# A linear-attention block times a GEGLU FFN: sums of fp32r passes recorded as three parts in free order, with a new schedule

## The chip, the core and the metric

The kernel runs on one core of one Trainium2 chip. The metric is the device time of one execution in microseconds (us), the median of several runs. The profile is of one execution; its span goes from the first to the last instruction of the core. The engines are named as in the profile: PE (TensorE), PEld (PE's weight loads), DVE (VectorE), ACT (ScalarE), POOL (GpSimd) and SP (SyncE, which issues the DMAs here).

## What is computed

The input x has 2048 tokens of 512 features. Two results are made of it, and out = x + s * silu(g):

```python
def _A_ref(x, wqkv, wo):            # s = _A_ref(_layernorm(x), wqkv, wo), 32 heads of 16
    ...
    phi = lambda t: jnp.where(t > 0, t + 1, jnp.exp(t)) + 1e-6
    pq, pk = phi(q), phi(k)
    kv = jnp.einsum("bhsd,bhse->bhde", pk, v)
    z = jnp.einsum("bhsd->bhd", pk)
    num = jnp.einsum("bhqd,bhde->bhqe", pq, kv)
    den = jnp.einsum("bhqd,bhd->bhq", pq, z)[..., None] + 1e-6
    o = num / den
    return (lambda x, *d: x.transpose(*d))(o, 0, 2, 1, 3).reshape(B, S, D) @ wo

def _B_ref(x, w_gate, w_up, w_down):  # F = 1792
    return (_gelu(x @ w_gate) * (x @ w_up)) @ w_down

s = _A_ref(xn, A_wqkv, A_wo)
g = _silu(_B_ref(xn, B_w_gate, B_w_up, B_w_down))
return x + s * g
```

## The kernel before

**Heads and tails.** Every large product is of fp32 accuracy, made of fp32r passes. `split` (L350, L356) makes of a matrix a head (ACT casts it to fp32r) and a tail (DVE or POOL subtracts the head from the matrix). `mm3` (L362 to L366) then adds three passes to one PSUM bank, always in this order: head by head (L364), head by tail (L365), tail by head (L366). A pass is 128x128 weights against 128x512 moving elements.

**Stages on PE.** Warm-up matmuls on ones (L387) stand first: four to bank 7 and eleven to bank 0. Tiles of 128 tokens are normalised (`ln`: bn_stats, bn_aggr and the rest on DVE, the power on POOL), transposed by PE (`pt`, L522, four transposes of 128x128) and split into Xh and Xl, or b for the differences that a product scheme needs. The first two groups of two token tiles get plain products: `k00`, `k01`, `k10`, `k11`, then q. All further groups, and the FFN's gate and up products, use a scheme of seven half-size products for a 2x2 block product (`prod` L555, `fprod` L797, `quad` L830), whose partial sums are named X, Y, Z (FX, FY, FZ in the FFN). X stays open: it is copied out by ACT (`e`, `u`, `fe`, `fu`) between products that go on adding to it. `gacc` (L612) adds k's features times the tokens to four banks (`gps`), from which the attention matrix M is made later. The FFN runs twice, for the second half of the tokens (p=1) and then for the first (p=0), each over seven units of the hidden dimension. `down` (L868) makes eight sums of 128x512 for each of the groups [0], [1,2], [3,4], [5,6] of units, named `d`; ACT copies the first group's out, DVE adds the later ones to `acc` (L885). Between the two halves stands the attention stage (`attn`): for each of 16 token tiles POOL makes u, DVE makes den, its reciprocal rr, and pn; PE transposes pn (`ptq`), ACT and DVE split it (`pqTh`, `pqTl`), and twelve passes make `sps`. `finish0` (L1060 on) closes p=0: silu on ACT, a multiply on DVE, an add of x (POOL for j below 6, else DVE) and the DMA of the output. The last sum of all, j=7 of the last group, is one sum of 12 passes; what follows it is done in two halves of 256 columns.

**The order.** All operations are recorded with their dependences by `Plan.do`. `Plan.order` keeps PE's operations in the order of a key list that is written out (`pe_keys`), and places those of ACT, DVE, POOL and SP by a list schedule with a cost for each operation. Eight rounds of latest times and forward passes are followed by 400 random alterations of the latest times, of which an alteration is kept if the planned end isn't later. Each `mm3` group of two or four terms is one operation, so the passes of a sum stay together and in one order. What the engines execute is fixed by the resulting program; the engines wait for each other by semaphores.

## Time and profile before

| | |
|---|---|
| timed runs, median (lowest to highest) | 632.24 us (632.04 to 632.71), 3 runs |
| the profiled execution's own time | 629.64 us |
| its span, first to last instruction | 627.6 us |
| instructions | 7822 |
| mean granted PE clock | 0.998 |
| DMA | 68.67 MB, 109 GB/s over the span |

The profiled execution lies 2.6 us below the median of the timed runs, and 2.04 us of it lie around its span. A line of the timeline gives the start in the span, the duration, the engine, the source line and operation, the tile written and the tiles read, the shape, and how many alike follow one another; in brackets stands how long the engine was idle before it and what ended the idle time. Ends of matmuls are modelled, so a pass shows 0.39 us though the next one starts earlier; the pace of PE is read from start to start.

### The profile page before, as it was taken

To read this page: it belongs to the slowest core of one execution; us is meant where nothing else is said; L and a number is where in the kernel's file an instruction comes from. 1 tells how busy PE (TensorE), PEld (TensorE's weight loads), DVE (VectorE), ACT (ScalarE), POOL (GpSimd) and SP (SyncE) were. 2 spreads that over 40 slices of the span, in tenths; PEclk is the share of its full clock that TensorE was granted. 3 is DMA by queue.
4 is the path that set the end of the run, shared out by engine and by line. 5 is a ranking of instruction groups with operands and counts; after the bars stand their busy time and mean duration, and the time that the engine had idled before them with its cause. 6 is when DMAs were issued, how large, how long until landed. Compare 5 with 4: busy or idle time off the path is not lost.

```text
span 627.6 us, 7822 instructions
## 1 busy us (share of the span) xinstructions
PE 616.1 (98%) x2780; PEld 506.0 (81%) x2780; DVE 422.2 (67%) x644; ACT 321.2 (51%) x571; POOL 247.9 (40%) x243
## 2 busy tenths in 40 slices
PE   7999999999999999999999999999999999999995
PEld 6878788888888888888888787888888888888884
DVE  6999998688746743762459689967566527723554
ACT  6677777797565622650345322266656316612431
POOL 2465554456644530360035433135534404300142
PEclk9999999999999999999999999999999999999999
DMA  6239921136121210220069544872221202000173
GB/s 239 80 124 299 298 68 38 65 102 201 44 72 54 56 46 34 67 68 0 34 201 359 199 131 148 289 251 67 68 65 36 68 34 68 0 1 34 34 206 130
DMA packets 52439, 68.67 MB, mean 109 GB/s; under 512 B 2864, under 2 KB 31792, under 8 KB 52400
## 3 DMA queue, kind: packets, MB, share of 16 engines
q1 hardware_dynamic: 52400, 68.17, 33.9%
q8 instruction: 22, 0.36, 0.2%
q14 instruction: 17, 0.14, 0.1%
HBM read 49.28 MB, written 18.87 MB: 109 GB/s over the span
## 4 chain that ended last, share of the span: by engine, by line
PE 94%; DVE 3%; ACT 1%; issue 0%; POOL 0%; DVEq 0%; ACTq 0%; POOLq 0%
PE FX L364 8%; PE FX L365 8%; PE FX L366 8%; PE d L365 8%; PE d L366 8%; PE d L364 8%; PE FZ L365 4%; PE FZ L366 4%; PE FZ L364 4%; PE sps L366 2%; PE sps L364 2%; PE sps L365 2%; PE gps L366 2%; PE gps L364 2%; PE gps L365 2%; PE FY L365 2%
## 5 line engine op out<-in xcount | busy, mean ns | idle before, releaser
L847 POOL TENSOR_TENSOR h<-h,g 128x512 f32<-128x512 f32 x42 | 62.1, 1477 | 173.3 <-DVE h L356 173.3
L364 PE MATMUL d<-dwh,hh 128*128 128x512 f32 x224 | 87.8, 392 | 0.0
L364 PE MATMUL FX<-Xh,w 128*128 128x512 f32 x224 | 87.5, 391 | 0.1
L366 PE MATMUL FX<-Xh,w 128*128 128x512 f32 x224 | 87.2, 389 | 0.0
L366 PE MATMUL d<-dwh,hl 128*128 128x512 f32 x224 | 87.2, 389 | 0.0
L365 PE MATMUL d<-dwl,hh 128*128 128x512 f32 x224 | 87.2, 389 | 0.0
L365 PE MATMUL FX<-Xl,w 128*128 128x512 f32 x224 | 87.2, 389 | 0.0
L356 POOL TENSOR_TENSOR tmp<-raw 128x256 f32<-128x256 f32 x56 | 49.1, 890 | 85.1 <-DVE w L356 70.3
L885 DVE TENSOR_TENSOR acc<-acc,d 128x512 f32<-128x512 f32 (+1 forms) x49 | 32.8, 674 | 52.5 <-PE d L366 52.1
L350 ACT COPY fu<-FX 128x512 f32<-128x512 f32 x56 | 32.9, 587 | 54.3 <-PE FX L366 53.7
L350 ACT CAST hh<-h 128x512 fp32r<-128x512 f32 x56 | 34.5, 620 | 46.4 <-PE d L365 27.0
L364 PEld LDWEIGHTS FX<-Xh,w 128*128 128x128 f32 x224 | 42.0, 188 | 10.0 <-ACT fu L350 1.4
L364 PEld LDWEIGHTS d<-dwh,hh 128*128 128x128 f32 x224 | 42.1, 188 | 8.9 <-issue 0.2
L365 PEld LDWEIGHTS d<-dwl,hh 128*128 128x128 f32 x224 | 42.1, 188 | 8.8 <-issue 0.2
L366 PEld LDWEIGHTS d<-dwh,hl 128*128 128x128 f32 x224 | 42.0, 188 | 8.7
L366 PEld LDWEIGHTS FX<-Xh,w 128*128 128x128 f32 x224 | 42.0, 188 | 8.7
L365 PEld LDWEIGHTS FX<-Xl,w 128*128 128x128 f32 x224 | 42.0, 188 | 8.7
L356 DVE TENSOR_TENSOR w<-tmp,w 128x512 fp32r<-128x512 f32 x56 | 42.0, 772 | 9.8 <-ACT w L350 9.8
L356 DVE TENSOR_TENSOR w<-raw,w 128x512 fp32r<-128x512 f32 (+1 forms) x56 | 45.7, 825 | 3.2 <-ACT w L350 3.2
L356 DVE TENSOR_TENSOR hl<-h,hh 128x512 fp32r<-128x512 f32 x56 | 41.2, 735 | 5.6 <-ACT hh L350 5.6
L364 PE MATMUL FZ<-Xh,w 128*128 128x512 f32 x112 | 43.6, 389 | 0.0
L365 PE MATMUL FZ<-Xl,w 128*128 128x512 f32 x112 | 43.6, 389 | 0.0
(186 smaller groups left out, 1396.8 us busy)
## 6 DMA issues: line engine op xcount, KB each, us to landing
raw<-in_B_w_gate SPq DMA_DIRECT2D x14, 512.0 KB, 3.8
raw<-in_B_w_up SPq DMA_DIRECT2D x14, 512.0 KB, 3.8
draw<-in_B_w_down SPq DMA_DIRECT2D x14, 512.0 KB, 3.3
x<-in_A_x SPq DMA_DIRECT2D x16, 256.0 KB, 3.3
q_d<-qp SPq DMA_DIRECT2D x16, 256.0 KB, 2.2
q<-q_d SPq DMA_DIRECT2D x16, 256.0 KB, 3.0
xh_d<-Xh SPq DMA_DIRECT2D x4, 896.0 KB, 5.9
xl_d<-Xl SPq DMA_DIRECT2D x4, 896.0 KB, 6.4
```

Of the source, the lines that this page charges most:

```text
L350: do("ACT", act(n), lambda o, i: nc.scalar.copy(o, i), dst, src, name=name)
L356: do(eng, c, lambda o, p, q: getattr(e, f"tensor_{op}")(o, p, q), dst, a, b, name=name)
L364: nc.tensor.matmul(ps, wh, mh, start=start, stop=False, skip_group_check=on)
L365: nc.tensor.matmul(ps, wh, ml, start=False, stop=False, skip_group_check=on)
L366: nc.tensor.matmul(ps, wl, mh, start=False, stop=stop, skip_group_check=on)
L847: do("POOL", pool(NC), lambda o, i: nc.gpsimd.tensor_mul(o, o, i), h, g, name="h")
L885: do("DVE", dve(D // n), lambda o, i: nc.vector.tensor_add(o, o, i), acc[p, j][cl], ps[cl], name="acc")
```

## The change

**Passes.** `mm3` goes. A class `Sum` records the passes of a sum in three parts, each an operation of its own: all head-by-head passes, all head-by-tail, all tail-by-head. Parts of one sum have no order among themselves (a resource keeps the sum it belongs to, and what was there before it), and the first pass that is made starts the bank. For this the heads and tails of k, q, w and M become separate resources, so a part waits only for what it reads. Where several terms or several `gps` banks stand together, `by_part` puts the first parts of all ahead of the second and third ones. Apart from the last sum the number of passes stays as it was.

**The plan.** The 400 random alterations are replaced by two short lists of numbered ones (`KEPT`), each limited to a stretch of PE time. [...] All other engines' orders come out anew.

**The start.** The four warm-up matmuls to bank 7 and one of the eleven others go. `ln` of the first tile is recorded ahead of the splits of the weights, and of the first group's second tile apart; the second tile of x is now the second DMA of SP's queue, ahead of k's weights. The tails of the second of each two row blocks of k's weights are made on POOL.

**The end.** The last sum of p=0 is made in two halves of 256 columns in two banks, 12 passes of 128x256 each, and its add, silu, multiply, add and output follow for each half. `finish0` adds x on DVE for every j.

```diff
-ROUNDS = 400
-WARM = 11
+KEPT = [
+    (-1, 12, [3200031, 3200084, 3200113, 3200368]),
+    (605, 9999, [3200013, 3200102, 3200161, 3200247]),
+]
...
+PASS, SHORT = 0.2267, 0.12
+WARM = 10
...
         for r in outs:
-            op.pre.update(r.writers)
-            op.pre.update(r.readers)
-            r.writers, r.readers = [op], []
+            if sum is None or r.sum is not sum:
+                r.before = {*r.writers, *r.readers}
+                r.writers, r.readers, r.sum = [], [], sum
+            op.pre.update(r.before)
+            r.writers.append(op)
...
-        draw = random.Random(1)
-        for n in range(ROUNDS):
-            end, done, late = best
-            for o in self.ops:
-                o.late = late[o]
-            waits = self.waits(done)
-            at = draw.choices([w[0] for w in waits], [w[1] for w in waits])[0]
-            back, share, far = draw.uniform(1.0, 12.0), draw.choice((0.05, 0.2, 0.5)), draw.uniform(0.2, 4.0)
+
+        for lo, hi, draws in KEPT:
+            for n in draws:
+                best = self.altered(n, lo, hi, pe, *best)
+        return [o for _, o in best[1]]
...
+                    for g in o.banks:
+                        p = last.get(g)
+                        if p and p.eng != e:
+                            t = max(t, p.end + p.lat)
+                    o.turn_at = t
...
+            if o.table and o.table != table:
+                t, table = t + LOAD, o.table
+
+            took = o.cost - (min(self.CUT[o.eng], t - asked) if o.port else 0.0)
+
+            if o.eng == "PE" and t > free["PE"] + 0.02:
+                took += 0.1
+            free[o.eng] = o.end = t + took
+            for g in o.banks:
+                if g in last and last[g].eng != o.eng:
+                    o.behind.append(last[g])
+                last[g] = o
...
-    def mm3(ps, wh, wl, mh, ml, start, stop, on=False):
-
-        nc.tensor.matmul(ps, wh, mh, start=start, stop=False, skip_group_check=on)
-        nc.tensor.matmul(ps, wh, ml, start=False, stop=False, skip_group_check=on)
-        nc.tensor.matmul(ps, wl, mh, start=False, stop=stop, skip_group_check=on)
+    subs = {}
+
+    class Sum:
+
+
+
+        def __init__(self, ps, on=False):
+            self.ps, self.on, self.passes, self.made = ps, on, 0, 0
+
+        def add(self, key, *parts, name="", cost=PASS):
+
+            for n, part in enumerate(parts):
+                self.passes += len(part)
+
+                def run(o, *v):
+                    for a, b in zip(v[::2], v[1::2]):
+                        self.made += 1
+                        nc.tensor.matmul(o, a, b, start=not self.on and self.made == 1,
+                                         stop=self.made == self.passes, skip_group_check=self.on)
+                do("PE", cost * len(part), run, self.ps, *[v for ab in part for v in ab],
+                   key=(*key, "part", n), name=name, sum=self)
+                subs.setdefault(key, []).append((*key, "part", n))
+
+    def three(ws, ms):
+
+        return ([(w[0], m[0]) for w, m in zip(ws, ms)], [(w[0], m[1]) for w, m in zip(ws, ms)],
+                [(w[1], m[0]) for w, m in zip(ws, ms)])
...
-    do("PE", 1.3, lambda o, w: warm(o, w, 4), bank(7, "warm2", (P, P)), ones, key="warm2")
...
+    ln(tokens[0][0])
     for k in range(2):
-        kq_split(0, wk1, k)
+        kq_split(0, wk1, k, eng="POOL" if k else "DVE")
     for k in range(2):
-        kq_split(1, wk2, k)
+        kq_split(1, wk2, k, eng="POOL" if k else "DVE")
...
+    def by_part(keys):
+
+        pe_keys.extend(subs[key][n] for n in range(3) for key in keys)
+
     def g_take(k):
-        for _ in range(min(k, len(g_todo))):
-            pe_keys.append(g_todo.pop(0))
+        by_part([g_todo.pop(0) for _ in range(min(k, len(g_todo)))])
...
-    pe_keys += [("T", 0, 0), "warm2"]
+    pe_keys.append(("T", 0, 0))
     for m, (n, i) in enumerate(tiles):
         plain_keys("K", n, i)
         if m + 1 < len(tiles):
-            pe_keys.insert(-2, ("T", *tiles[m + 1]))
+            pe_keys.insert(-5, ("T", *tiles[m + 1]))
...
-        wv = w.part(w.res[g:g + 1], (slice(None), slice(None), slice(2 * a, 2 * a + 2)))
-        xv = [xrows(hl, b, b + 1) for hl in "hl"]
-
-        def run(o, w, xh, xl):
-            for k in range(2):
-                mm3(o, w[:, 0, k], w[:, 1, k], xh[:, k], xl[:, k], start and k == 0, k == 1, not start)
-        do("PE", 1.36, run, ps, wv, *xv, key=("F", q, i), name="fprod")
+        wh, wl = (w.part(w.res[4 * hl + g:4 * hl + g + 1], (slice(None), hl, slice(2 * a, 2 * a + 2))) for hl in range(2))
+        xh, xl = (xrows(hl, b, b + 1) for hl in "hl")
+        Sum(ps, not start).add(("F", q, i), *three([(wh[:, k], wl[:, k]) for k in range(2)],
+                                                   [(xh[:, k], xl[:, k]) for k in range(2)]), name="fprod")
...
+    def halves(p, units_, j):
+
+        return 2 if p == 0 and units_ == groups[-1] and j == 7 else 1
+
     def down(p, units_, is_first, is_last, finish):
         for j in range(8):
             key = (11, 21) if j < 4 else (12, 22)
             sl = slice((j % 4) * P, (j % 4 + 1) * P)
-            ps = bank(ring("down", [5, 6, 7]), f"d{p}_{units_[0]}_{j}")
-            for n, u in enumerate(units_):
-                for i in range(2):
-                    def run(o, hh, hl, dh, dl, sl=sl, i=i, st=(n == 0 and i == 0), sp=(n == len(units_) - 1 and i == 1)):
-                        mm3(o, hh[:, sl], hl[:, sl], dh[:, i], dl[:, i], st, sp)
-                    do("PE", 0.68, run, ps, *hs[p, u, key[i]], *dws[p, u], key=("D", p, u, j, i), name="down")
+            m = halves(p, units_, j)
             if is_first:
-                acc[p, j] = tile_in("up", FACC[j], [P, D], F32, f"acc{p}_{j}")
-                copy("ACT", acc[p, j], ps, D, "acc")
-            else:
-                n = 2 if p == 0 and is_last and j == 7 else 1
-                for i in range(n):
-                    cl = (slice(None), slice(i * D // n, (i + 1) * D // n))
-                    do("DVE", dve(D // n), lambda o, i: nc.vector.tensor_add(o, o, i), acc[p, j][cl], ps[cl], name="acc")
+                acc[p, j] = tile_in("up", FACC[j], [P, D], F32, f"acc{p}_{j}", 2 if halves(p, groups[-1], j) > 1 else 1)
+            for c in range(m):
+                ps = bank(ring("down", [5, 6, 7]), f"d{p}_{units_[0]}_{j}{c}", (P, D // m))
+                cs = slice(c * D // m, (c + 1) * D // m)
+                total = Sum(ps)
+                for u in units_:
+                    hh, hl = hs[p, u, key[0]], hs[p, u, key[1]]
+                    dh, dl = dws[p, u]
+                    total.add(("D", p, u, j, c), *three([(h[0][:, sl], h[1][:, sl]) for h in (hh, hl)],
+                                                       [(dh[:, i, cs], dl[:, i, cs]) for i in range(2)]),
+                              name="down", cost=PASS if m == 1 else SHORT)
+                a = columns(acc[p, j], c, m)
+                if is_first:
+                    copy("ACT", a, ps, D, "acc")
+                else:
+                    do("DVE", dve(D // m), lambda o, i: nc.vector.tensor_add(o, o, i), a, ps, name="acc")
...
     def finish0(p, j):
-        n = 2 if j == 7 else 1
-        sr, xr = U("fs", [*FG, *FX], f"fs{j}"), U("fxr", [*FE, *FC], f"fx{j}")
+        n = halves(p, groups[-1], j)
+        sr = U("fs", [*FG, *FX], f"fs{j}", parts=n)
+        xr = U("fxr", [*FE, *FC], f"fx{j}")
         dma(sr, s_d(j, slice(j * P, (j + 1) * P)), 256)
         dma(xr, ext(x[j * P:(j + 1) * P, :]), 256)
         w = D // n
         silu(p, j, n)
         for i in range(n):
-            cl = (slice(None), slice(i * w, (i + 1) * w))
-            do("DVE", dve(w), lambda o, a: nc.vector.tensor_mul(o, o, a), sr[cl], acc[p, j][cl])
-            tt("POOL" if j < 6 else "DVE", "add", sr[cl], sr[cl], xr[cl], w)
-            dma(ext(out[j * P:(j + 1) * P, i * w:(i + 1) * w]), sr[cl], 256 // n)
+            so = columns(sr, i, n)
+            do("DVE", dve(w), lambda o, a: nc.vector.tensor_mul(o, o, a), so, columns(acc[p, j], i, n))
+            tt("DVE", "add", so, so, xr[:, i * w:(i + 1) * w], w)
+            dma(ext(out[j * P:(j + 1) * P, i * w:(i + 1) * w]), so, 256 // n)
```

The first place is PE's first rows: `pt0` and `pt4` are the transposes of the first two token tiles, `k00` and `k01` the first two k tiles, `kq0` k's weights (heads and tails), `b12` the differences made for the second tile. Before:

```order
L387 MATMUL warm2_99<-ones_88 128x128 x4
L387 MATMUL warm_118<-ones_88 128x128 x11
L522 MATMUL pt0_154<-ident_90,xn0_149 128x128 x4
L522 MATMUL pt4_181<-ident_90,xn4_177 128x128 x4
L364 MATMUL k00_190<-kq0_175,Xh0_165 128x512
L365 MATMUL k00_190<-kq0_175,Xh0_165 128x512
L366 MATMUL k00_190<-kq0_175,Xl0_170 128x512
```

And in the changed kernel, in the same place:

```order
L490 MATMUL warm_96<-ones_88 128x128 x10
L624 MATMUL pt0_150<-ident_111,xn0_143 128x128 x4
L460 MATMUL k00_173<-kq0_167,Xh0_163 128x512
L624 MATMUL pt4_176<-ident_111,xn4_165 128x128 x4
L460 MATMUL k00_173<-kq0_167,Xh0_163 128x512
L460 MATMUL k00_173<-kq0_167,Xl0_182 128x512
L460 MATMUL k00_173<-kq0_167,Xh0_163 128x512
L460 MATMUL k01_195<-kq0_167,b12_0_189 128x512
L460 MATMUL k00_173<-kq0_167,Xl0_182 128x512
```

The first k pass has moved ahead of the second tile's transposes, the extra warm-up is gone, and passes of k00 and k01 alternate.

The second place is PE in the last quad of p=1's FFN, where FX13 is copied out by ACT and goes on being added to after a piece of a down sum (`d1_5_0`). `hh11_11` and `hl11_11` are head and tail of the hidden values, `dwh1_5` and `dwl1_5` of the down weights. Before:

```order
L364 MATMUL FX13_2988<-Xh0_165,w13_2688 128x512
L365 MATMUL FX13_2988<-Xl0_170,w13_2688 128x512
L366 MATMUL FX13_2988<-Xh0_165,w13_2688 128x512
L364 MATMUL d1_5_0_3073<-dwh1_5_2881,hh11_11_2818 128x512
L365 MATMUL d1_5_0_3073<-dwl1_5_2886,hh11_11_2818 128x512
L366 MATMUL d1_5_0_3073<-dwh1_5_2881,hl11_11_2823 128x512
L364 MATMUL FX13_2988<-Xh0_165,w13_2688 128x512
```

In the changed kernel:

```order
L460 MATMUL FX13_2986<-Xh0_163,w13_2682 128x512 x2
L460 MATMUL d1_5_00_3070<-dwh1_5_2874,hh11_11_2812 128x512
L460 MATMUL d1_5_00_3070<-dwh1_5_2874,hh21_11_2954 128x512
L460 MATMUL d1_5_00_3070<-dwl1_5_2880,hh11_11_2812 128x512
L460 MATMUL d1_5_00_3070<-dwl1_5_2880,hh21_11_2954 128x512
L460 MATMUL FX13_2986<-Xh0_163,w13_2682 128x512 x2
```

Four down passes instead of three stand between the two stretches of FX13, since the head-by-head and the tail-by-head parts of both terms go first.

The third place is the end of DVE's row. `acc0_6` and `acc0_7` are the last two accumulators of p=0, `fs` the product with s, `fx` the input tile that is added. Before:

```order
L885 TENSOR_TENSOR acc0_6_4286<-acc0_6_4286,d0_5_6_5534 128x512
L1069 TENSOR_TENSOR fs6_5490<-fs6_5490,acc0_6_4286 128x512
L356 TENSOR_TENSOR fs6_5490<-fs6_5490,fx6_5468 128x512
L885 TENSOR_TENSOR acc0_7_4311<-acc0_7_4311,d0_5_7_5552 128x256 x2
L1069 TENSOR_TENSOR fs7_5505<-fs7_5505,acc0_7_4311 128x256
L356 TENSOR_TENSOR fs7_5505<-fs7_5505,fx7_5487 128x256
```

In the changed kernel:

```order
L983 TENSOR_TENSOR acc0_6_4280<-acc0_6_4280,d0_5_60_5527 128x512
L983 TENSOR_TENSOR acc0_7_4294<-acc0_7_4294,d0_5_70_5537 128x256
L1165 TENSOR_TENSOR fs6_5491<-fs6_5491,acc0_6_4280 128x512
L1165 TENSOR_TENSOR fs7_5509<-fs7_5509,acc0_7_4294 128x256
L983 TENSOR_TENSOR acc0_7_4294<-acc0_7_4294,d0_5_71_5562 128x256
L437 TENSOR_TENSOR fs6_5491<-fs6_5491,fx6_5462 128x512
L1165 TENSOR_TENSOR fs7_5509<-fs7_5509,acc0_7_4294 128x256
L437 TENSOR_TENSOR fs7_5509<-fs7_5509,fx7_5483 128x256 x2
```

The first half's add and multiply have moved ahead of the second half's add, and both halves' closing adds stand last.

More of the change, by code (lines that the diff above doesn't have):

```diff
@@ L70 @@
 class Op:
-    __slots__ = ("eng", "cost", "lat", "fn", "pre", "suc", "key", "late", "end", "left", "ready", "name", "turn", "port", "kb", "lat0")
+    __slots__ = ("eng", "cost", "lat", "fn", "pre", "suc", "key", "late", "end", "left", "ready", "name", "turn", "port", "kb", "lat0", "no", "table", "banks", "behind", "turn_at")
 class Plan:
     AHEAD = 6.0
-    RATE = 260.0
+    RATE = 220.0
+    CUT = {"DVE": 0.13, "POOL": 0.04}
     HOP = {"PE": 0.21, "ACT": 0.15, "DVE": 0.13, "POOL": 0.09, "SP": 0.0}
@@ L88, in do @@
         op.pre, op.suc, op.kb = set(), [], kb
-        op.port = eng == "POOL" or eng == "DVE" and cost > 0.25 and not any(
+        op.port = eng == "POOL" or eng == "DVE" and port and not any(
             isinstance(v, View) and v.psum for v in (out, *ins))
@@ L109, in do @@
                 v.gen.ops.add(op)
+        op.banks = [v.gen for v in (out, *more, *ins) if isinstance(v, View) and v.psum and eng != "PE"]
         op.pre.discard(op)
@@ L143, in order @@
                     o.late += draw.uniform(-far, far)
[L144 to L148 removed]
+        new = self.forward(pe)
+        return max(t for t, _ in new), new, {o: o.late for o in self.ops}
     @staticmethod
@@ L156, in waits, with chain @@
                 if t - o.cost - last > 0.02:
-                    out.append((o.late, t - o.cost - last))
+                    out.append((o.turn, t - o.cost - last, o))
                 last = t
-        out.append((last, max(t for t, _ in done) - last - 4.0))
+        t, o = max(done, key=lambda d: d[0])
+        out.append((o.turn, t - last, o)) if o.eng == "PE" else out.append((1000.0, t - last, o))
+        return out
+    def chain(self, done, o):
+        end = {q: t for t, q in done}
+        for q in self.ops:
+            q.lat = q.lat0 + q.kb / self.RATE
+        before, last = {}, {}
+        for t, q in done:
+            before[q] = last.get(q.eng)
+            last[q.eng] = q
+        out = []
+        for _ in range(14):
+            out.append(o)
+            held = [(end[q] + self.gap(q, o), q) for q in {*o.pre, *o.behind}]
+            if before[o]:
+                held.append((end[before[o]], before[o]))
+            if not held:
+                break
+            o = max(held, key=lambda h: (h[0], h[1].no))[1]
         return out
@@ L185, in latest @@
         free = dict.fromkeys(self.HOP, total)
-        port = total
+        port, turns = total, {}
+        if capacity:
+            for o in self.ops:
+                for q in o.behind:
+                    turns.setdefault(q, []).append(o)
         for o in reversed(done):
@@ L189, in latest @@
             if capacity:
+                for q in turns.get(o, ()):
+                    end = min(end, q.late - o.lat)
                 end = min(end, free[o.eng])
@@ L206, in forward @@
         for o in self.ops:
-            o.left, o.ready, o.end, o.lat = len(o.pre), 0.0, None, o.lat0
+            o.left, o.ready, o.end, o.lat, o.behind = len(o.pre), 0.0, None, o.lat0, []
         cands = {e: [] for e in self.HOP}
@@ L213, in forward @@
                 cands[o.eng].append(o)
-        done, first = [], 0
+        done, first, table, last = [], 0, "exp", {}
         while any(cands.values()):
@@ L676 @@
         if n == 0:
[L677 to L678 removed]
+            ln(tokens[n][1])
         else:
@@ L1076 @@
         pe_keys += last0(j)
-    for o in plan.order(pe_keys):
+    for o in plan.order([part for key in pe_keys for part in subs.get(key, [key])]):
         o.fn()
```

160 lines of the change are left out of this document (83 added, 77 removed).

## The prediction

> **What bounds the kernel now.** I read the page first, then TensorE's own waits, then the timeline around each wait, at the start and at the end.
>
> ```profile
> span 627.6 us, 7822 instructions
> ...
> PE 616.1 (98%) x2780; PEld 506.0 (81%) x2780; DVE 422.2 (67%) x644; ACT 321.2 (51%) x571; POOL 247.9 (40%) x243
> ...
> PEclk9999999999999999999999999999999999999999
> ...
> PE 94%; DVE 3%; ACT 1%; issue 0%; POOL 0%; DVEq 0%; ACTq 0%; POOLq 0%
> ...
> PE pt L522 <- DVE xn L510: 2.0, 1, 2.0
> PE Y L364 <- DVE qp L591: 0.5, 1, 0.5
> PE X L366 <- DVE Xl L356: 0.4, 1, 0.4
> ```
>
> TensorE (PE) is busy 98% of the span at full clock, and the chain that ended last is PE for 94%. So only three things can shorten this kernel: fewer passes, an earlier first pass with a shorter tail, or closing PE's gaps. The change hardly touches the first: each sum is still three passes per term, only in another order. What is left is small, because the recorded waits are a handful of microseconds. The profiled run took 629.64 us, 2.04 around its span; the median of the three timed runs is 632.24. All terms below are differences from the profiled run, and I take the same sum off the median.
>
> **The start.** Columns of a timeline row: start, duration, engine, line, tile.
>
> ```profile
> 1.12 2.29 PE L387 MATMUL warm<-ones 128*128 128x128 f32 x9 [1.12 <-DVE neg_half L378]
> ...
> 4.83 1.39 PE L387 MATMUL warm<-ones 128*128 128x128 f32 x11
> ...
> 7.23 2.24 ACT L350 CAST kq<-wk 128x512 fp32r<-128x512 f32 x4
> ...
> 8.50 2.49 DVE L356 TENSOR_TENSOR kq<-wk,kq 128x512 fp32r<-128x512 f32 x4
> ...
> 9.05 0.47 PE L364 MATMUL k<-kq,Xh 128*128 128x512 f32 x1
> ...
> 14.10 0.66 PE L522 MATMUL pt<-ident,xn 128*128 128x128 f32 x4
> 14.51 0.47 PE L364 MATMUL k<-kq,Xh 128*128 128x512 f32 x1
> ...
> 15.17 1.68 POOL L602 TENSOR_TENSOR zacc<-zacc,kp 128x512 f32<-128x512 f32 x1 [1.72 <-DVE kp L591]
> ...
> 22.06 0.39 PE L364 MATMUL q<-a,Xh 128*128 128x512 f32 x1
> ...
> 618.18 0.39 PE L364 MATMUL d<-dwh,hh 128*128 128x512 f32 x1
> ...
> 620.68 0.39 PE L366 MATMUL d<-dwh,hl 128*128 128x512 f32 x1
> ```
>
> The pace of a full pass comes from the last sum: its first pass starts at 618.18, its twelfth at 620.68, so 2.50/11 = 0.227 us each. A group of four transposes takes 14.51 - 14.10 = 0.41, and I add 0.1 for the slower pass after it. Between the first k pass (9.05) and the first q pass (22.06) PE makes the four k tiles, 48 x 0.227 = 10.90, and two transpose groups, 1.02: 11.92 of work in 13.01 us, so 1.09 of waits. In the changed order the second token tile's transposes no longer stand before the first k pass. A k sum may open with its head-by-head pass as soon as the first head cast is done; one cast is 2.24/4 = 0.56 in a row starting at 7.23, and the changed order puts one half-cast less ahead of it, so I put the first pass at 7.65. From there PE has the same 48 passes and now three groups, 12.43, ready at 20.08 without a wait. Half of k's tails now run on POOL, where the nearest row of that size takes 1.68, against 2.49/4 = 0.62 on DVE. I allow 0.7 of waits: q starts at 20.8, **-1.3**. Bounds: no wait at all gives -2.0. If the two POOL tails follow one another, 2 x 1.68 = 3.36 against the 1.24 they took on DVE, and all of that 2.1 is waited for on top of the 0.7, q starts at 22.9: +0.8.
>
> The rows that decide whether POOL can help are these.
>
> ```profile
> 57.94 3.04 POOL L356 TENSOR_TENSOR T<-xt,T 128x256 f32<-128x256 f32 x3
> 57.98 1.26 DVE L356 TENSOR_TENSOR Xl<-T,Xh 128x512 fp32r<-128x512 f32 x1 [0.21 <-ACT Xh L350]
> 59.17 1.22 DVE L591 SCALAR_TENSOR_TENSOR qp<-c,qr 128x512 f32<-128x512 f32 x1
> ```
>
> While POOL ran three operations, two DVE ones of a size that elsewhere takes 0.62 to 0.69 took 1.26 and 1.22, and POOL's three took 3.04. So the two engines delay each other: moving a tail to POOL doesn't free a whole DVE slot.
>
> [...]
>
> The warm-up is shorter as well: four of the fifteen warm matmuls are dropped and one of the eleven others. Two records belong to one, so 30 become 20. The first nine took 2.29 us (0.24 each), the eleven from 4.83 on 1.39, or 0.11 to the next start: PE ran at about half pace until some three microseconds after its first matmul. The shorter warm-up ends near 4.9 instead of 6.2. PE then waits for the first transposes. I cost this at nothing, because the 2.0 us wait for xn in the waits above was followed by passes at full pace. If the pace is lost, a second stretch like the first, 3 us at half pace, costs 1.5.
>
> [...]
>
> **The middle.** PE's gaps, and the pace of the attention stage:
>
> ```profile
> 43.22 0.39 PE L366 MATMUL X<-kq,Xl 128*128 128x512 f32 x1
> ...
> 44.14 0.50 PE L364 MATMUL Y<-kq,Xh 128*128 128x512 f32 x1 [0.53 <-DVE qp L591]
> ...
> 63.96 0.39 PE L365 MATMUL X<-kq,Xh 128*128 128x512 f32 x1
> ...
> 64.78 0.50 PE L366 MATMUL X<-kq,Xl 128*128 128x512 f32 x1 [0.43 <-DVE Xl L356]
> ...
> 326.92 0.39 PE L366 MATMUL d<-dwh,hl 128*128 128x512 f32 x1
> 327.36 0.50 PE L364 MATMUL FX<-Xh,w 128*128 128x512 f32 x1
> 327.70 0.39 PE L365 MATMUL FX<-Xl,w 128*128 128x512 f32 x1
> ...
> 425.56 0.39 PE L366 MATMUL FZ<-Xh,w 128*128 128x512 f32 x1
> 425.93 0.50 PE L364 MATMUL FX<-Xh,w 128*128 128x512 f32 x1
> ...
> 382.06 0.48 PE L364 MATMUL sps<-M_hi,pqTh 128*128 128x512 f32 x1
> ...
> 395.65 0.48 PE L364 MATMUL sps<-M_hi,pqTh 128*128 128x512 f32 x1
> ...
> L1012 DVE SCALAR_TENSOR_TENSOR pn<-q,rr x16: 672/692/1780, 342.6 to 403.2; 128x512 f32<-128x512 f32 x16
> ...
> 60.00:80.00 20.00, 19.57 (x90) 15.65 (x89) 19.73 (x34) 15.37 (x29) 11.04 (x11) 1.00 0.94 283
> ...
> 360.00:380.00 20.00, 20.00 (x101) 16.51 (x100) 17.73 (x32) 5.64 (x10) 5.45 (x4) 1.00 0.46 135
> ```
>
> A gap costs its length beyond 0.227, and 0.11 more, because the first pass after it takes 0.34 (327.36 to 327.70).
> - Bank loops. At 327.36 FX needs the bank that ACT is still copying out; three down passes stand between. Gap 0.44 - 0.227 = 0.21, with the slower pass 0.32. The second FFN half repeats this loop in the same order, so 0.64 for both. In the changed order four down passes stand there, which is 0.227 more cover than the 0.21 that lacks, so both go: **-0.6** (bounds -0.64 and 0).
> - Gaps behind DVE at 43.22 (0.92 - 0.227 + 0.11 = 0.80) and 63.96 (0.82 - 0.227 + 0.11 = 0.70). DVE reaches both later than PE wants. In the changed order DVE's qp stands earlier, but PE also comes about 1.3 us earlier, and DVE is busy 19.73 of 20 us here (third busy figure in the windows rows). I keep 0.5 of the 1.50: **-1.0** (bounds -1.5 and, with as much again, +1.5).
> - The gap at 425.56, 0.37 - 0.227 + 0.11 = 0.25, stands behind a gate chain on ACT and DVE; a 128x1024 weight tail that ran ahead of it on DVE now comes later: **-0.2** (bounds -0.25, 0).
> - Attention. One token tile costs PE 12 x 0.227 + 0.41 + 0.1 = 3.23, so four cost 12.9; from 382.06 to 395.65 four took 13.59, 0.7 lost to one late pn. The changed order has the den and pn of each tile earlier on DVE, but two weight tails now stand in this stage, and DVE was busy 17.73 of 20. I take **-0.3** (bounds -0.7, +0.7).
>
> **The tail.**
>
> ```profile
> 621.17 0.74 DVE L885 TENSOR_TENSOR acc<-acc,d 128x256 f32<-128x256 f32 x2
> 621.61 0.75 ACT L895 ACTIVATE acc<-acc 128x256 f32<-128x256 f32 x2 [1.87 <-DVE acc L885]
> ...
> 622.12 0.43 DVE L1069 TENSOR_TENSOR fs<-fs,acc 128x256 f32<-128x256 f32 x1 [0.21 <-issue]
> 623.37 0.42 DVE L356 TENSOR_TENSOR fs<-fs,fx 128x256 f32<-128x256 f32 x1
> ...
> 8.64 0.42 PEld L522 LDWEIGHTS pt<-ident,xn 128*128 128x128 f32 x4 [2.22 <-DVE xn L510]
> ```
>
> Before, both halves of the last sum are done at once: two adds, two silus, then two multiplies and two adds on DVE, four steps in 623.37 + 0.42 - 622.12 = 1.67. Now the first half is finished twelve half passes earlier, and its add, silu and multiply lie beside PE. The last pass starts half a pass later than before and is half a pass shorter, so the second half's add still starts at 621.17, its silu 0.44 later, its multiply at 622.12; only this multiply and the two closing adds follow, at 1.67/4 = 0.42 a step or somewhat less: 623.3 to 623.4 instead of 623.79, **-0.5**. The passes of 128x256 aren't in the trace. If one takes half a full pass, 0.113, nothing is added; if it costs as much as a full one, 24 x 0.113 = 2.7 is. The nearest rows are the transposes, 128 columns each, at about 0.11, whose four weight loads fit in 0.42: I take 0.113. Bounds of the tail: -0.7 (steps of 0.35) and +2.2. The six closing adds moved from POOL to DVE (0.69 each) lie beside the last sums; uncovered, the last one would cost 0.7.
>
> **The sum** is -1.3 - 0.6 - 1.0 - 0.2 - 0.3 - 0.5 = -3.9. The order is new throughout, and I have read it only at these places. I allow 0.3 for one new gap of the size of those above: **-3.6**, so 626.0 against the profiled run and **628.6** against the median.
>
> **The rivals.**
> 1. DVE sets the pace of the early part. For: 19.73 of 20 us busy. Then the 1.3 of the start and the 1.0 behind DVE are lost again before 100 us, and the loops, 425, attention and tail remain: -1.6, 630.6.
> [...]
> 3. Cold start: PE loses its pace after the short warm-up, +1.5 on the forecast: 630.1. Against: full pace after the 2.0 us wait.
> 4. It doesn't do what it says: the free order only trades gaps for others, since passes neither vanish nor shorten. Total unchanged but for some tenths: 631.9. Against: the bank loops and the tail are arithmetic on rows, 1.1 together.
> 5. Slower: the attention stage becomes DVE's. DVE has 17.73/20 x 3.23 = 2.86 us of work a tile, 0.37 to spare. Were every pn stretched like the worst (1.78 instead of 0.69), a tile would need 3.95, 0.72 over PE, 16 tiles 11.5 us: 640. It makes the kernel slower from (3.9 - 0.3 + 1.26)/16 = 0.30 over PE a tile, a stretch of 0.67 on each. Against: the median pn is 0.692, and it would take most of the sixteen.
>
> **How the numbers follow.** Within 0.2% (1.26 us, about what a measurement of this kernel can tell from no change) means 630.98 to 633.50. Forecast 0.54 (own range 627.0 to 630.0), DVE pace 0.13, port at the start 0.07, cold start 0.06, no effect 0.12, DVE-bound attention 0.08. The first four are faster, 0.80; same 0.12; slower 0.08. With every gain at its bound the sum would be -5.8, 626.4, to which I give 0.07 below 626.9. Above 631.5 lie half of the no-effect case and all of the slow one, 0.14. So the range is 626.9 to 631.5.
>
> **What would show it.** Right: q starts near 20.8; no FX gap near 326 and 596; the gap before Y near 43 gone; the last half passes 0.113 apart; the last add ending 2.5 us after the last pass starts. Wrong: first k passes 0.4 apart (cold); DVE rows over 1.2 us beside POOL's k tails and q after 22; ptq waiting for pn at several tiles; half passes near 0.2.

## The result, and the profile after

| | before | changed |
|---|---|---|
| first measurement, median (lowest to highest), 4 runs each | 632.45 us (632.04 to 632.71) | 626.02 us (625.18 to 627.05) |
| ratio, 95% interval | | 0.990 (0.9882 to 0.9917) |
| again on another chip, 17 and 6 runs | 630.50 us (629.76 to 632.78) | 625.96 us (625.32 to 627.26), ratio 0.9925 (0.9906 to 0.9945) |
| the profiled execution's own time, its span | 629.64, 627.6 us | 625.18, 623.2 us |

The changed kernel is 6.4 us faster by the first measurement, 4.5 by the second, and 4.46 from profile to profile; 3.6 was forecast. One thing is needed to read these numbers: executions of the kernel before lie in two groups some 2 us apart, and by their times all four of its first timed runs lay in the upper one. What the groups are is found below.

The page, and PE's waits, of the changed kernel:

```profile
span 623.2 us, 7828 instructions
...
PE 615.2 (99%) x2782; PEld 506.1 (81%) x2782; DVE 408.5 (66%) x648; ACT 319.1 (51%) x571; POOL 233.0 (37%) x239
...
PE 98%; DVE 0%; DMA 0%; ACT 0%; issue 0%; POOL 0%; DVEq 0%
...
PE warm L490 <- DVE neg_half L481: 1.1, 1, 1.1
PE k L460 <- ACT kq L431: 1.0, 1, 1.0
PE pt L624 <- DVE xn L576: 0.2, 1, 0.2
```

The waits of Y and X behind DVE and of sps behind ACT are gone from the list; what is left stands in the first 8 us. Where the 4.37 us of span went, by the start of the same PE work in the two profiles:

| stage | before | changed | gained |
|---|---|---|---|
| first q pass | 22.06 | 20.77 | 1.29 |
| first FX pass | 136.07 | 133.27 | 1.51 more |
| PE's last pass starts, plus its pace (0.227; 0.12) | 620.91 | 617.42 | 0.69 more |
| last output lands | 625.53 | 622.07 | -0.03 |
| span's end | 627.58 | 623.21 | 0.91 more |

Timeline rows of the changed kernel that answer to those of before (start, duration, engine, line, tile):

```profile
7.61 0.50 PE L460 MATMUL k<-kq,Xh 128*128 128x512 f32 x1 [0.98 <-ACT kq L431]
...
8.67 3.04 POOL L437 TENSOR_TENSOR kq<-wk,kq 128x512 fp32r<-128x512 f32 x2 [1.83 <-ACT kq L431]
...
20.77 0.61 PE L460 MATMUL q<-a,Xh 128*128 128x512 f32 x2
...
324.57 0.61 PE L460 MATMUL d<-dwl,hh 128*128 128x512 f32 x2
325.02 0.72 PE L460 MATMUL FX<-Xh,w 128*128 128x512 f32 x2
325.58 0.62 PE L460 MATMUL FX<-Xl,w 128*128 128x512 f32 x2
...
616.94 0.40 PE L460 MATMUL d<-dwl,hh 128*128 128x256 f32 x2
617.18 0.40 PE L460 MATMUL d<-dwh,hl 128*128 128x256 f32 x2
617.62 0.42 DVE L983 TENSOR_TENSOR acc<-acc,d 128x256 f32<-128x256 f32 x1
...
618.66 1.73 SPq L427 DMA_DIRECT2D out_y<-fs  x3
618.89 0.75 DVE L437 TENSOR_TENSOR fs<-fs,fx 128x256 f32<-128x256 f32 x2
```

The first k pass and the first q pass stand where they were forecast (7.65 and 20.8). FX follows the down passes at the usual pace (two in 325.02 - 324.57 = 0.45), but its first pair takes 0.56 instead of 0.45: the gap is gone, the slower pass isn't. A half pass takes (617.18 - 616.94)/2 = 0.12.

### The profile page after: what moved, and what is told of

The parts are those of the page before. It is cut to its first block, busy times and chain, and to the rows that moved or that the text cites. A ratio compares the mean times of both kernels' runs of the same rounds, so it can differ in the third digit from the quotient of the medians.

```text
span 623.2 us, 7828 instructions
## 1 busy us (share of the span) xinstructions
PE 615.2 (99%) x2782; PEld 506.1 (81%) x2782; DVE 408.5 (66%) x648; ACT 319.1 (51%) x571; POOL 233.0 (37%) x239
## 4 chain that ended last, share of the span: by engine, by line
PE 98%; DVE 0%; DMA 0%; ACT 0%; issue 0%; POOL 0%; DVEq 0%
PE FX L460 25%; PE d L460 24%; PE FZ L460 12%; PE sps L460 7%; PE gps L460 7%; PE FY L460 6%; PE X L460 5%; PE Z L460 3%; PE k L460 2%; PE q L460 2%; PE Y L460 1%; PE pt L624 1%; PE ptq L1115 1%; PE pkv L1075 1%; PE pm L1087 1%; DMA x<-in_A_x 0%
## 5 line engine op out<-in xcount | busy, mean ns | idle before, releaser
L460 PE MATMUL FX<-Xh,w 128*128 128x512 f32 x448 | 134.4, 391 | 0.0
L437 POOL TENSOR_TENSOR tmp<-raw 128x256 f32<-128x256 f32 x56 | 45.0, 822 | 93.0 <-DVE w L437 77.9
L460 PE MATMUL d<-dwh,hh 128*128 128x512 f32 (+1 forms) x228 | 69.7, 388 | 0.0
L460 PE MATMUL d<-dwh,hl 128*128 128x512 f32 (+1 forms) x228 | 69.2, 385 | 0.0
L460 PE MATMUL FX<-Xl,w 128*128 128x512 f32 x224 | 69.1, 390 | 0.0
L460 PE MATMUL FZ<-Xh,w 128*128 128x512 f32 x224 | 69.0, 389 | 0.0
L460 PE MATMUL d<-dwl,hh 128*128 128x512 f32 (+1 forms) x228 | 68.9, 385 | 0.0
L460 PEld LDWEIGHTS FZ<-Xh,w 128*128 128x128 f32 x224 | 42.1, 188 | 8.7
L431 ACT CAST dwh<-draw 128x1024 fp32r<-128x1024 f32 x14 | 14.7, 1049 | 47.3 <-PE d L460 45.1
L437 DVE TENSOR_TENSOR g<-fu,FZ 128x512 f32<-128x512 f32 x28 | 19.1, 683 | 30.0 <-PE FZ L460 27.0
```

Source lines behind the costliest of these rows:

```text
L431: do("ACT", act(n), lambda o, i: nc.scalar.copy(o, i), dst, src, name=name)
L437: do(eng, c, lambda o, p, q: getattr(e, f"tensor_{op}")(o, p, q), dst, a, b, name=name)
L460: nc.tensor.matmul(o, a, b, start=not self.on and self.made == 1, stop=self.made == self.passes, skip_group_check=self.on)
```

## Experiments

"Order kept" means: the operations are issued in exactly the order that the plan of the changed kernel (or of the kernel before) gave, written into the kernel as a list, so that only the named edit differs.

### The two kernels again

> The kernel before, unchanged, profiled once more. The two profiles differ by 4.4 us of span, the medians of the timed runs by 6.4. Theory A: the first profile of before was a lucky execution (629.64 against 632.04 to 632.71 timed), and a second one has a span near 630 us, with the 2 to 2.6 us that are missing in one or two places of PE's timeline (a wait at the start, or waits behind DVE between 40 and 100 us). Rival B: a profile of before is always some 2.5 us faster than its timed runs, and the new span is 627.6 again within 0.5 us; then the gain that the timed runs show has a part that no profile can.

> The changed kernel, unchanged, profiled once more. Its four runs lay between 625.18 and 627.05. Theory A: its spread is of the same kind as that of before, at one or two places, and the new span lies between 623 and 625 us. Rival: its spans are all alike within 0.3 us on one chip, and the spread is between chips. Ratio to before 0.988 to 0.992 in both.

Before: span 628.1 in the profile, 12 runs from 630.03 to 632.87. Each timed run gives its span and its mean granted PE clock. Of 86 timed runs of before on four occasions, 34 had a clock of 0.995 or 0.996 and took 631.7 us or more; the other 52, at 0.997 to 0.999, took 629.6 to 631.4. Neither theory had the reason: the first profile was no lucky one but of the larger group. The changed kernel: span 623.6, runs from 625.32 to 627.26 without such a step.

### k's tails on DVE again, and 15 warm-up matmuls (both with the order kept)

```diff
-        kq_split(0, wk1, k, eng="POOL" if k else "DVE")
+        kq_split(0, wk1, k)
...
-        kq_split(1, wk2, k, eng="POOL" if k else "DVE")
+        kq_split(1, wk2, k)
```

> The changed kernel with its order kept, only the two tails of k that it moved to POOL made on DVE again, at the same place of the order. If POOL's help makes part of the 1.3 us at the start, the first q pass comes 0.5 to 1.3 us later than 20.77 and the time is up by as much (626.5 to 627.3 where the changed kernel takes 626.0). [...]

627.04 us, ratio to before 0.9938 (0.9919 to 0.9957), q at 22.00. From the first k pass to the first q pass PE took 13.95 us, against 13.16 with the tails on POOL (20.77 - 7.61); the rest of the delay, 0.4, stood ahead of the first k pass, where PE was still at half pace (the four transposes from 6.02 took 1.05, against 0.66 from 5.97 in the changed kernel). In all eight profiles that have the changed kernel's order and POOL's tails this stretch took 13.12 to 13.17. One wait carries most of the difference, a new one on the tail (the three passes from 12.88 to 14.14 take 1.26 instead of 0.68):

```profile
12.86 0.66 DVE L513 TENSOR_TENSOR kq<-wk,kq 128x512 fp32r<-128x512 f32 x1
12.88 0.40 PE L536 MATMUL k<-kq,Xh 128*128 128x512 f32 x1
...
13.57 0.50 PE L536 MATMUL k<-kq,Xh 128*128 128x512 f32 x1 [0.29 <-DVE kq L513]
```

So POOL's tails carry 0.8 of the 1.3 at the start. The timed runs alone don't show it: the interval overlaps that of the changed kernel (0.9906 to 0.9945).

```diff
-WARM = 10
+WARM = 15
```

> The changed kernel with its order kept and 15 warm-up matmuls instead of 10, as many as before had. In the profile of the changed kernel the passes between 8.34 and 9.69 us are 0.34 apart instead of 0.23. If that is PE's pace lost after the short warm-up, they are 0.23 apart here and the first q pass comes up to 0.5 us earlier, unless a tail is waited for then; the time falls by 0 to 0.5 us. If each of these passes has waited a moment for its data, the spacing stays and the time is the same within 0.2 us.

626.40 us (625.75 to 626.57). The spacing of 0.34 stays (9.09, 9.42, 9.76, 10.10), so it isn't a lost pace; the granted clock reads 1.00 there in both profiles. That each of those passes waited a moment for its data is what is left, and isn't shown alone. In the profile the longer warm-up held the first k pass back to 8.36, and its six runs lie closer together: 0.8 us from lowest to highest, against 1.9.

### The end and the bank loop (order kept)

The last sum as one sum of 12 passes, with the add and all behind it in halves as before:

```diff
-            for c in range(m):
-                ps = bank(ring("down", [5, 6, 7]), f"d{p}_{units_[0]}_{j}{c}", (P, D // m))
+            ps = bank(ring("down", [5, 6, 7]), f"d{p}_{units_[0]}_{j}")
...
+            for c in range(m):
+                a = columns(acc[p, j], c, m)
...
+                    do("DVE", dve(D // m), lambda o, i: nc.vector.tensor_add(o, o, i), a,
+                       ps[:, c * D // m:(c + 1) * D // m], name="acc")
```

> The changed kernel with its order kept up to the end, but the last sum is one sum of 12 passes again, with add, silu, multiply and add in halves behind it, as before. The trace of the changed kernel has the last add end 2.2 us after PE's last pass starts plus a pass, 0.77 us nearer than before. If the halves are what did this, the distance between the last pass and the last add grows by 0.6 to 0.9 us and the time by as much. If the adds moved from POOL and the earlier end of the sixth sum's work did it, the time grows by less than 0.3 us. PE's own end stays within 0.1 us, since a half pass was 0.12 apart.

625.80 us, ratio 0.9915 (0.9894 to 0.9936): no loss that the runs can tell. The last add is 0.72 further from PE's end, as expected, but the span's end only 0.18 (5.97 against 5.79). The end of this run, with the row of its output DMAs:

```profile
618.19 0.75 DVE L1056 TENSOR_TENSOR acc<-acc,d 128x256 f32<-128x256 f32 x2
618.30 2.83 SPq L502 DMA_DIRECT2D out_y<-fs  x3
...
620.34 0.42 DVE L512 TENSOR_TENSOR fs<-fs,fx 128x256 f32<-128x256 f32 x1
```

Here SP's last issue starts at 620.79, right after the last add (620.76). In the changed kernel the three issues start at 618.66, 619.34 and 620.07. The first two follow their data at once (ready at 618.64 and 619.31); the last stands 0.43 behind its data, although the issue before it ended at 619.67, and it then takes 2.0 to land instead of 1.7 before. The two together use up what the halves gained.

In the last quad of each FFN half, one down operation of two passes behind the first two FX passes:

```diff
 d1_5_00 <- dwh1_5, hh11_11 and hh21_11
-d1_5_00 <- dwl1_5, hh11_11 and hh21_11
 FX13 <- Xh0, w13 (two passes)
+d1_5_00 <- dwl1_5, hh11_11 and hh21_11
```

> The changed kernel with its order kept, but in the last quad of each FFN half one down operation of two passes goes behind the first two FX passes instead of ahead of them, so two passes instead of four stand between ACT's copy and the next FX pass. By the bank loop as I priced it (0.21 us short with three passes, 0.11 for the slower pass after it) two passes lack 0.44 and cost 0.55 at each of the two places: 1.1 us in all. Rival: PE's 0.33 step after the copy, which the changed kernel still shows at 325.0 and 593.6, already is the whole cost, and the time grows by less than 0.4.

627.05 us, 1.1 over 625.96 (measured on another chip), ratio 0.9933 (0.9914 to 0.9952). In its timeline, with two passes between:

```profile
324.29 0.61 PE L536 MATMUL d<-dwh,hh 128*128 128x512 f32 x2
324.54 0.58 ACT L507 COPY fu<-FX 128x512 f32<-128x512 f32 x1 [1.15 <-PE FX L536]
...
325.18 0.74 PE L536 MATMUL FX<-Xh,w 128*128 128x512 f32 x2 [0.28 <-ACT fu L507]
325.76 0.63 PE L536 MATMUL d<-dwl,hh 128*128 128x512 f32 x2
```

Two passes and the gap take 325.18 - 324.29 = 0.89, 0.44 more than two passes, and the next pair 0.58 instead of 0.45, which is the price as worked out. Against the changed kernel each of the two places costs only 0.48 (the first FZ pass behind them starts 0.66 later where the passes ahead of them start 0.18 later, then 1.23 against 0.75), because its own first pair takes 0.56 too. So four passes instead of two remove the gap, and not the slower pass.

### What the two groups are

The kernel before with 10 warm-up matmuls (WARM 6 plus the four to bank 7), its order unchanged:

> The kernel before with 10 warm-up matmuls instead of 15, its order unchanged. Its runs lie in two groups, 629.8 to 630.9 and 631.3 to 632.9. Theory A: the groups come from the moment at which PE's pace doubles, which was 4.3, 5.4, 5.5 to 6, and over 6.7 us in five profiles; while it is late, the 15 warm-up matmuls run up to 7.5 us and hold the first transposes back. Then with 10 the warm-up ends by 5.4 in any case, and the upper group gets rarer or lies less than 1.5 above the lower. Rival B: the groups come from a race later on, between DVE and POOL, and stay as they are: 0.3 to 0.6 of the runs over 631.3.

> The kernel before with 10 warm-up matmuls once more, for a profile: nine of its twelve runs lay over 631.3 us, with a mean granted clock of 0.993 to 0.996. By the revised theory A the passes between some 8.5 and 12 us are 0.43 apart instead of 0.23 in such a run, and all later stages lie about 1.3 to 2 us later than in the fast profile of before. By rival B the time is lost at a gap after 40 us, with the start unchanged.

631.90 us; nine of twelve runs at 0.993 to 0.996 and over 631.3. The shorter warm-up made the upper group larger, against theory A as it stood. The second of its profiles, with a clock of 0.995, fell into it: transposes at 8.58 to 9.28 0.21 apart instead of 0.11, and passes 0.43 apart up to 11.2.

Nine more matmuls on ones in the idle time between the two transposes of before, and four in that of the changed kernel (order kept, results not used):

```diff
+    do("PE", 2.0, lambda o, w: warm(o, w, 9), bank(7, "fill", (P, P)), ones, key="fill")
```

> The kernel before with its order kept and nine more matmuls on ones (about 2 us) in PE's idle time between the first and the second token tile's transposes; their results are not used. Theory A, revised: some 40% of the runs of before are about 2 us longer because PE's pace is halved once more for some 3.4 us after this idle time; those runs show a mean granted clock of 0.995 to 0.996 instead of 0.998 to 0.999, and 0.003 of 628 us is 1.9 us. With the gap filled these runs get rare (at most 1 in 10 over 631.3), the median falls to 630.0 to 630.5, and the fast group stays at 629.8 to 630.9. Rival B, a race between DVE and POOL later on: the share of such runs stays at 0.3 to 0.5.

> The changed kernel with its order kept and four more matmuls on ones in PE's idle time between the first transposes and the first k pass; their results are not used. Its idle times here are 0.6 and 1.1 us against the 2.0 of before. Theory A: the changed kernel owes part of its gain to the shorter idle time, its slow runs (627.0 to 627.3, one in five) are the same thing, and they go; the spread shrinks to under 1 us and the median is 625.3 to 625.9. If PE is still at half pace when the filler comes, it takes 1.7 instead of 0.9 and the first k pass is 0.6 late, so a run can also be 626.5. Rival B: no difference, 626.0 with runs up to 627.3.

Before, filled: twelve runs from 630.59 to 631.68, all at 0.998 or 0.999, where 11 of 23 runs of before on the same chip had 0.996 and lay between 631.71 and 632.82. The upper group is gone. The median, 630.99, is no lower than before's on that chip (630.74), because the filled runs lie some 0.9 above its lower group. Why they do isn't shown: in the profile the first k pass stands at 9.86, but 2.99 behind the first transposes, just as in before, since the warm-up ended later. Changed, filled: 625.89 us, 625.37 to 626.65, six runs without one near 627. That the runs near 627 were such runs, as theory A had it, the clocks don't bear out: 627.05 had 1.0 and 627.26 had 0.998, where the 3.4 us at half pace of the last profile below alone would make it 0.997, by my estimate (1.7 of 627).

Three more profiles of the kernel before:

> The kernel before, one more profile. If it falls in the upper group (span over 629.2), its timeline shows where the 2 us lie: by theory A all before the first q pass, by rival B at a gap behind DVE between 40 and 140 us or in the attention stage. In the lower group it says nothing new.

> The kernel before, one more profile. In about four of ten runs it falls in the slow group (span over 629.5, mean granted clock 0.995 to 0.996). Then, by the theory of the lost pace, its passes are 0.43 apart over some 3.4 us between 8.5 and 13, the first q pass starts 1.3 to 2 us later than 22.06, and all later stages lie as much later, with no other change. By the rival, a race later on, q starts within 0.7 of 22.06 and the loss stands between two later stages. In the fast group it adds nothing.

> The same once more, with the same expectation: the slow group shows passes 0.43 apart near 8.5 to 13 us (theory), or a loss after 40 us (rival); the fast group adds nothing.

The first two had clocks of 0.999 and 0.998 and q at 22.24 and 22.72; the second also waited once more for a pn in the attention stage. The last one has a span of 629.9 and a clock of 0.996. Its start, and PE's windows (PE busy, PEld, DVE, ACT, POOL, then the granted clock):

```profile
9.73 0.93 PE L522 MATMUL pt<-ident,xn 128*128 128x128 f32 x4 [1.98 <-DVE xn L510]
10.31 0.78 PE L364 MATMUL k<-kq,Xh 128*128 128x512 f32 x1
10.88 0.63 PE L365 MATMUL k<-kq,Xh 128*128 128x512 f32 x1
11.31 0.63 PE L366 MATMUL k<-kq,Xl 128*128 128x512 f32 x1
...
13.02 0.57 PE L364 MATMUL k<-kq,Xh 128*128 128x512 f32 x1
13.42 0.39 PE L365 MATMUL k<-kq,Xh 128*128 128x512 f32 x1
13.66 0.39 PE L366 MATMUL k<-kq,Xl 128*128 128x512 f32 x1
...
8.00:12.00 4.00, 2.27 (x8) 1.98 (x9) 3.54 (x8) 3.81 (x10) 0.00 (x0) 0.75 1.04 389
12.00:16.00 4.00, 4.00 (x16) 3.11 (x16) 3.34 (x10) 2.58 (x6) 0.70 (x1) 0.83 0.09 36
```

The clock drops inside the transposes at 10.0 and is back at 13.4: passes 0.43 apart, then 0.23. In this execution the warm-up reached full pace only at 6.59 (with the first transposes it ended at 7.75, against 6.66 in the first profile), which makes the first k pass 1.26 late; the second loss makes q 2.25 late (24.31), and every later stage is 2.2 to 2.3 late. That is the upper group.

In this trace the pace is lost 3.42 us after the first full pace and is back 3.41 later (6.55, 9.97 and 13.38 in the trace's clock; the clocks of 0.75 and 0.83 above say the same, 2.0 us at half pace up to 12.00 and 1.36 behind it). The profiles differ in how much of PE's idle time falls into the first 3.4 us at full pace: by the modelled ends 1.0 to 1.8 us in the five profiles of before, and of before with 10 warm-up matmuls, that kept the pace, and 2.0 and 2.1 us in the two that lost it. In before the latest full pace and the second loss stand in the same execution. That this idle time decides it isn't shown: the changed plan without draws, below, lost the pace with 1.4 us.

### The free order and the draws

Passes in fixed order (head by head, head by tail, tail by head, term after term; terms that are added together, as the two of a down sum for one unit, are one operation of six passes):

```diff
         def add(self, key, *parts, name="", cost=PASS):
-
+            parts = [[p for term in zip(*parts) for p in term]]
...
-        pe_keys.extend(subs[key][n] for n in range(3) for key in keys)
+        pe_keys.extend(subs[key][0] for key in keys)
...
-            pe_keys.insert(-5, ("T", *tiles[m + 1]))
+            pe_keys.insert(-2, ("T", *tiles[m + 1]))
```

> The changed kernel without the free order: the passes of each term stand together again, head by head, head by tail, tail by head, as one operation for the plan, which is made anew; all else (costs, kept draws, tails on POOL, halves) stays. If the free order carries the gain at the start and at the bank loops, q starts 0.8 to 1.3 us later than 20.8, the FX gaps of 0.44 come back (0.3 each), and the time is 627.5 to 629. Rival: the new costs and the start's order carry it, and the time is within 0.5 us of 626.0.

631.56 us: the whole gain gone, and more than expected; q starts at 22.54, 1.8 late. The FX gaps did not come back: six down passes stand there in this plan, where before had three. But the draws were chosen for another plan. So the same pair without draws (`KEPT = []`):

> The changed kernel without the eight kept draws, planned anew; free order, costs, tails on POOL and halves stay. The draws work on the first 12 us and the end alone. If they carry the start's gain, q starts 0.5 to 1.5 us later than 20.8 and the time is 626.5 to 628; if the free order does it by itself, 626 to 626.5.

> Passes in fixed order and no kept draws, planned anew; costs, tails on POOL and halves stay. The difference from the free order without draws is what the free order is worth: 2 to 5 us if it carries the gain (629 to 631.5 here), under 1 us if the fixed order of the earlier run only suffered from draws chosen for another plan.

Free order 627.04 us, ratio 0.9935 (0.9915 to 0.9954); fixed order 629.61, ratio 0.9983 (0.9971 to 0.9995). On this chip before took 630.08, so of the 3.0 us that the plan without draws gains, the free order is worth 2.6; the new costs, the start and the halves leave 0.5 without it, and none of the costs was taken back alone. What the kept draws are worth isn't shown: 627.04 against 625.96 is 1.1, but on different chips, with intervals that overlap. In the profile of the free one, with a clock of 0.996, PE was at half pace from 8.8 to 12.2 (three passes from 10.46 on in 1.28, 0.43 each), which can account for the 1.3 by which its q (22.06) came late: the loss of pace isn't confined to before. The profile of the fixed one, with 0.993, was at half pace from 8.4 to 15.2, so their starts can't be compared. Behind the start, the fixed order made PE wait three times for ACT's `u`, 0.8 us in all, where the changed kernel shows no such wait:

```profile
PE X L457 <- ACT u L428: 0.8, 3, 0.3
```

### The end once more

Order kept, but the sixth tile's add and output, and the first half's, ahead of the second half's multiply; then the same with the filled gap:

```diff
 acc6, acc7 first half, mul6
+add6, out6
 acc7 second half, mul7 first half
+add7 first half, out7 first half
-add6
 mul7 second half
-add7 first half
 add7 second half
```

> The changed kernel with its order kept but for the end: the sixth tile's add and output stand right behind its multiply, ahead of the second half of the last sum, and the first half's multiply, add and output ahead of the second half's multiply. In the changed kernel three output DMAs follow one another on SP 0.7 us apart, and the last is issued at 620.07 though its data are ready at 619.64; one sum in place of two halves took no longer. If this queue takes the halves' gain back, the last DMA is issued within 0.1 us of the last add, the last add ends 0.1 to 0.3 earlier, and the time falls by 0.4 to 0.9 us (625.2 to 625.6 at the median). Rival: the end hangs on something else (landing of the DMAs, the program's end), and the time is within 0.2 us of the changed kernel's.

> Both edits together: the end reordered as in the run before, and four more matmuls on ones in PE's idle time between the first transposes and the first k pass (results not used). If each acts on its own, the median is 625.0 to 625.4 and the spread under 1.3 us, the fastest kernel of the study.

625.71 us, ratio 0.9918 (0.9899 to 0.9936), and 625.28 us (624.72 to 625.70), ratio 0.9908 (0.9891 to 0.9925). The last issue now follows the last add (620.08 after 620.05), but the add6 in between put that add 0.2 further from PE's end, and the landing still takes 2.0: 0.19 us nearer from PE's end to the span's end, the rival's size. Both edits together give the lowest median of the study, with 0.98 us from lowest to highest (only the 15 warm-up matmuls, with 0.82, did better there); the interval doesn't separate them from the changed kernel.

## Why the prediction was wrong, point by point

**The step that failed** is "I take the same sum off the median". The sum stands against a profiled execution in which PE kept its pace; 632.24 was the median of three executions that by their times all belong to the group in which PE lost it (of the 86 later runs of before, every one above 631.4 had a clock of 0.996 or less). I noted the 2.6 us between profile and median and didn't ask what they were. Set against the profile, the sum (-3.6) missed 4.46 by 0.9; set against a median of the upper group, which lies about 2 us higher, the forecast of 628.6 missed 626.02 by 2.6 and the range by 0.9. That all the first runs lay in that group was chance: at 34 in 86, four in a row come about once in 40 times, by my estimate. It is luck, too, that 626.0 against the profile is nearly the measured median. Up to the last landing the stages gained 3.46, close to 3.6, but by errors that cancel: 0.5 more than forecast in the gaps behind DVE, 0.4 less behind FX, 0.5 less in the tail, and 0.3 held back for new gaps.

**The cold-start rival** named the right mechanism and put it in the wrong kernel. I priced it for the changed one and took the 2.0 us wait of before, followed by full pace in one profile, as proof that such a wait costs nothing. By their clocks it did cost in 34 of 86 runs of before. Filling the wait removes these runs; that is shown (0.998 or 0.999 in all twelve). None of the nine profiles with the changed kernel's order lost the pace. That this is because its idle times are shorter (0.2 and 1.0 us in its list of waits) isn't shown: the plan without draws lost it with like ones (0.4 and 1.0).

**The start**, -1.3, measured -1.29, in the way that was worked out, but the hit is in part luck: q started at 22.06, 22.24, 22.59, 22.72 and 24.31 in five profiles of before, and I had the earliest; in two of the changed kernel it was 20.77 and 20.79. The tails on POOL carry 0.8 of it. POOL's two tails took 3.04 us, nearly the 3.36 of my bound, and a tail of DVE's beside them 1.05 instead of 0.69. But PE found other passes of the two sums to make in the meantime. No run shows the "port at the start" to which 0.07 went; what the trace shows is DVE's longer row, and q 1.29 earlier all the same.

**Gaps behind DVE**, -1.0, measured -1.51 between q and FX. Both are gone; I kept 0.5 for new ones, which came to some tenths, and left out a third gap, at 59.31 (0.39 to the next pass, which follows ACT's copy of X), a bank loop like FX13's.

**Bank loops, 425, attention**, -1.1 together, measured -0.69 (half passes cost 0.16 of it). The loop's mechanism is right, as the run with two passes shows (0.28 idle behind ACT's `fu`); but the slower pass after the copy stays (0.10 at 325.02 and 593.55), so each loop gave 0.21 and not 0.32, and single slower passes of that size are new at 163, 253 and 522.

**The tail**, -0.5. The last add came nearer to PE's end by 0.66 (2.88 to 2.22), but the last output was issued 0.43 after its data and landed 0.3 more slowly: 0.03 lost up to the landing. The halves were worth 0.2 at most (5.97 against 5.79 from PE's end), which the runs can't tell from nothing. I had followed the data to the last add and not the DMA behind it.

**What wasn't in the sum:** 0.91 us between the last landing and the end of the program.

The rivals of a DVE-paced early part, of no effect and of a DVE-bound attention stage didn't come about: after the first 8 us no wait stands in PE's list.

## What to carry to other kernels

A profiled execution and the median of the timed runs need not be the same state of affairs: where they lie apart by more than the effect, find out in which place before adding a sum to either. A PE idle time in the first ten microseconds can cost more than its length: in the last profile of before one of 1.98 us was followed by 3.4 us at half pace, and q, 1.26 late up to there, came 2.25 late. So look at the pace of the first passes, not only at the waits. And a tail ends with the landing of its last DMA: here the last add came 0.66 nearer to PE's end, and the landing 0.03 further from it, because the output was issued and landed later.

## What the runs showed of the chip beside that

- The moment at which PE reached full pace differed from execution to execution with the same warm-up: 4.3, 4.7, 5.4, 5.7 and 6.6 us in profiles of before (first matmul at 1.12; in four of them warm-up and first transposes ended at 6.66, 6.84, 7.17 and 7.75), and 6.4 to 6.9 in four of the changed kernel's variants.
- From the last output's landing to the end of the span, all profiles of before and its variants took 2.05 us and those of the changed kernel with its order kept 1.14; the plans without draws took 1.17 and the plan with fixed order and draws 1.47. Nothing of the edit is meant for this stretch. In before two steps of SP's closing exchange (625.92 to 626.25, 626.70 to 627.52) are 0.3 and 0.45 us longer than in the changed kernel; the cause stays open.
- The last of three output DMAs on SP started 0.73 us after the one before it in the changed kernel, though that issue shows 0.33 us and the data had been ready for 0.43; in the plan with fixed order and no draws it started 0.44 after. What holds it isn't shown.
